# Query transposes by DMA instead of TensorE in a fused pooled-attention and gated-FFN kernel, with a thinner second chunk

## Chip, cores, metric

One core of a Trainium2 chip. The metric is the device time of one execution in microseconds (us), lower is better. Kernels that are compared ran in the same rounds on the same chip. A ratio is the mean time of one kernel's fast runs over the mean of the other's fast runs of the same rounds, so it is not quite the ratio of the medians that are quoted. Spans and times inside a run are from one profiled execution of each kernel.

## The reference, cut to what matters

```python
# q, k, v: [8 batches, 8 heads, 576, 64] float32
k_p = k.reshape(B, H, 72, 8, D).mean(axis=3)      # keys and values pooled by 8
v_p = v.reshape(B, H, 72, 8, D).mean(axis=3)
attn = softmax(q @ k_p.T / sqrt(D))               # 576 x 72 per head
x = (attn @ v_p) as [4608 tokens, 512]
out = (relu(x @ w_gate) * (x @ w_val)) @ w_out    # 512 -> 1536 -> 512
```

## The kernel before

Everything is fp16 in SBUF. The 4608 tokens go through the FFN in 9 chunks of 512. While chunk c runs, the attention of batch c+1 is woven in piece by piece. Scores need the queries with the head dimension on the partitions; they arrive with it along the row, so each batch needs 18 transposes of 128x128, done on TensorE and copied out of PSUM by VectorE.

```python
def load_q(b, ...):                     # cast to fp16 on the way, issued by GpSimd; 2 buffers q16
    nc.gpsimd.dma_start(out=q16_tiles[b][:, cols], in_=flat[:, cols])

def q_transposes(b, n, eng):            # pieces q0, q1 (8 blocks each), q2 (2 blocks)
    if n == 0:
        qT_tiles[b] = qT_pool.tile([P, NI, P], F16, name="qT")          # 2 buffers
    i0, cnt = n * IQ, min(IQ, NI - n * IQ)
    ps = ps_mm.tile([P, IQ, P], F16, name="mm_ps", tag="mm_ps")
    for i in range(cnt):
        c0 = (i0 + i) * P
        nc.tensor.transpose(out=ps[:, i, :], in_=q16_tiles[b][:, c0:c0 + P], identity=ident16)
    ...                                 # copy ps to qT_tiles[b][:, i0:i0 + cnt, :]

def scores(b, h):                       # Sc[h]: 2 matmuls of 288 columns, one Exp on ACT
def values(b, h):                       # V[h]: 2 matmuls of 288 columns, Ln and Exp on ACT,
                                        #       2 multiplies on VectorE into x_T
def attention(b, nxt):
    Sc, V = scores_of(b), values_of(b)
    if nxt is None:
        return [V[0], Sc[2], V[1], ..., Sc[7], V[6], V[7]]               # 14 pieces
    (q0, q1, q2), kt = transposes_of(nxt)
    Sn = scores_of(nxt)
    return [V[0], q0, Sc[2], V[1], Sc[3], V[2], q1, Sc[4], V[3], Sc[5], V[4], kt, Sc[6], V[5],
            Sc[7], V[6], q2, V[7], Sn[0], Sn[1]]

def weave(units, others):               # pieces spread evenly over the units
    n, m = len(others), len(units)
    for i, unit in enumerate(units):
        unit()
        run(others[i * n // m:(i + 1) * n // m])

# chunk 0, tail (loads of the output weights and of batch 2 are issued just ahead of it)
run(z[0:6] + [a[6], q0, a[7], q1, z[6], q2, z[7], kt, a[8], Sc[0], a[9], Sc[1], ...])
...
for c in range(1, n_chunks):
    units = ...                         # 12 gate/value units; from chunk 2 on 8 output units too
    others = []
    if c + 1 < B:
        others = early + attention(c + 1, c + 2 if c + 2 < B else None)   # early: batch 2, chunk 1 only
        early = []
        if c + 2 < B:
            prep(c + 2, c + 3 < B)      # pooling of batch c+2 on GpSimd, loads of batch c+3
        else:
            others += [lambda: None] * 3                                  # fillers
    weave(units, others)
```

The softmax here doesn't subtract the row's maximum and nothing guards it: scores larger than these inputs give would overflow.

Of the kernel before, what the change touches and what calls it, by code (L numbers as in the profile page):

```python
# [10 lines left out]
F16 = mybir.dt.float16  # L11
# [5 lines left out]
def kernel(  # L17
# [10 lines left out]
    nc = tc.nc  # L28

    B, H, S, D = q.shape  # L30
# [5 lines left out]
    P = 128  # L36
# [9 lines left out]
    NI = QT // 2  # L46
# [14 lines left out]
    qT_pool = ctx.enter_context(tc.tile_pool(name="qT", bufs=2))  # L61
# [45 lines left out]
    k_tiles, v_tiles, q16_tiles = {}, {}, {}  # L107
# [56 lines left out]
    def run(pieces):  # L164
        for piece in pieces:
            piece()
# [7 lines left out]
    def k_windows(b, ps, w0, n):  # L174


        for w in range(w0, w0 + n):
            nc.tensor.transpose(
                out=ps[:, w, :],
                in_=kps[b % 2][:KROWS, w:w + 2, :].rearrange("p j d -> p (j d)"),  # L180
                identity=ident16[:KROWS, :KROWS])

    def k_evacuate(b, ps, upper, eng):

        ds, x, w = (slice(D, P), 1, 0) if upper else (slice(0, D), 0, 1)
        dst = kpTs[b % 2].rearrange("d h x (s j) -> d h x s j", j=KJ)[ds, :, x]
        src = ps.rearrange("d w (h s) -> d h s w", h=H)[ds, :, :, w:w + KJ]
        if eng is nc.scalar:
            eng.copy(dst, src)
        else:  # L190
            eng.tensor_copy(out=dst, in_=src)

    def k_transposes(b):
        ps = ps_mm.tile([P, KJ + 1, KROWS], F16, name="mm_ps", tag="mm_ps")
        k_windows(b, ps, 0, KJ + 1)
        for upper in (False, True):
            k_evacuate(b, ps, upper, nc.vector)

    qT_tiles = {}

    def q_transposes(b, n, eng):
        if n == 0:
            qT_tiles[b] = qT_pool.tile([P, NI, P], F16, name="qT")
# [5 lines that stand above are left out]
        dst = qT_tiles[b][:, i0:i0 + cnt, :]  # L209
        if eng is nc.scalar:  # L210
            eng.copy(dst, ps[:, :cnt])
        else:
            eng.tensor_copy(out=dst, in_=ps[:, :cnt])

    def queries(b, h, i0=0, n=NI):
        return qT_tiles[b][:, i0:i0 + n, h * QP:(h + 1) * QP]
# [3 lines left out]
    def scores(b, h):  # L220
        ps = ps_at.tile([P, 2, 512], F32, name="at_ps", tag="at_ps")
        for j in range(2):
            nc.tensor.matmul(  # L223
                out=ps[:SP, j, :HS], lhsT=kpTs[b % 2][:, h, j, :], rhs=queries(b, h),
                start=True, stop=True,
            )
        e = exp_pool.tile([P, 2, HS], F16, name="expT")
        nc.scalar.activation(out=e[:SP], in_=ps[:SP, :, :HS], func=AF.Exp, scale=EXP_SCALE)  # L228
        exp_tiles[b, h] = e
# [226 lines left out]
    def scores_of(b):  # L456
        return [lambda h=h: scores(b, h) for h in range(H)]

    def values_of(b):
        return [lambda h=h: values(b, h) for h in range(H)]  # L460

    def transposes_of(b):
        return [lambda n=n: q_transposes(b, n, nc.vector) for n in range(NQ)], \
            lambda: k_transposes(b)

    def attention(b, nxt):


        Sc, V = scores_of(b), values_of(b)
        if nxt is None:  # L470
            return [V[0], Sc[2], V[1], Sc[3], V[2], Sc[4], V[3], Sc[5], V[4], Sc[6], V[5], Sc[7],
                    V[6], V[7]]
        (q0, q1, q2), kt = transposes_of(nxt)
        Sn = scores_of(nxt)
        return [V[0], q0, Sc[2], V[1], Sc[3], V[2], q1, Sc[4], V[3], Sc[5], V[4], kt, Sc[6], V[5],
                Sc[7], V[6], q2, V[7], Sn[0], Sn[1]]

    def weave(units, others):

# [5 lines left out]
    with tc.manual_schedule():  # L485
        nc.scalar.preload_act_table_set("natural_log_exp_and_others")
        nc.vector.memset(warm_sb, 0.0)
        for kp in kps:
            nc.vector.memset(kp[:, 0, :], 0.0)
            nc.vector.memset(kp[:, KJ + 1, :], 0.0)  # L490
        for kpT in kpTs:
            nc.vector.memset(kpT[:D, :, 1, :], 0.0)
            nc.vector.memset(kpT[D:, :, 0, :], 0.0)
        for st in stats:
            nc.vector.memset(st[:SP, :, D:3 * D], ONE)
        load_k(0, parts=KJ // 2)
        make_identity(nc, ident16)
        load_q(0, 0, IQ)
        load_v(0, (0, D, SP))
        load_gv(0)  # L500
        load_q(0, IQ, NI - IQ)
        for i in range(1, 4):
            load_gv(i)
        load_k(1)
        load_gv(4)
        load_q(1)
        load_gv(5)
        load_v(1)

        for i in range(KJ // 2):  # L510
            run(pool_k(0, i, nc.vector))
        warm(12)
        k_ps = ps_mm.tile([P, KJ + 1, KROWS], F16, name="mm_ps", tag="mm_ps")
        k_windows(0, k_ps, 0, 2)
        warm(3)
        k_windows(0, k_ps, 2, 2)
        warm(2)
        q_transposes(0, 0, nc.scalar)
        k_windows(0, k_ps, 4, KJ - 3)
        k_evacuate(0, k_ps, False, nc.vector)  # L520
        k_evacuate(0, k_ps, True, nc.vector)
        warm(2)
        piece_scores(0)
        warm(2)
        piece_scores(1)
        warm(2)
        pool_v_array(0, 0)
        pool_v_array(0, 1)

        half = TCH // 2  # L530
        a = [lambda fo=fo: gate_val(0, fo, 0, half) for fo in range(n_fo)]
        z = [lambda fo=fo: gate_val(0, fo, half, half) for fo in range(n_fo)]
        piece_values(0)
        piece_values(1)
        warm(1)
        piece_back(0, nc.vector)
        warm(1)
        piece_back(1, nc.scalar)
        a[0]()
        q_transposes(0, 1, nc.scalar)  # L540
        piece_scores(2)
        a[1]()
        q_transposes(0, 2, nc.vector)
        piece_scores(3)
        a[2]()
        piece_values(2)
        piece_scores(4)
        a[3]()
        piece_back(2, nc.vector)
        piece_values(3)  # L550
        a[4]()
        piece_back(3, nc.scalar)
        piece_values(4)
        a[5]()
        piece_back(4, nc.vector)

        for i in range(KJ // 2):
            run(pool_k(1, i, nc.gpsimd))
        for i in range(3):
            load_wo(i, n_fo // 3)  # L560
        load_k(2)
        load_q(2)
        load_v(2)
        (q0, q1, q2), kt = transposes_of(1)
        Sc, V = scores_of(1), values_of(1)
        pv = [lambda half=half: pool_v_array(1, half) for half in range(2)]
        o = [p for ts in range(TCH // P) for p in out_rows(0, ts, nc.vector)]

        run(z[0:6] + [a[6], q0, a[7], q1, z[6], q2, z[7], kt, a[8], Sc[0], a[9], Sc[1], z[8], Sc[2],
                      z[9], Sc[3], a[10], Sc[4], a[11], Sc[5], z[10], Sc[6], z[11], Sc[7]])  # L570
        run(pv + [o[0], V[0], o[1], V[1], o[2], V[2], o[3], V[3], o[4], V[4], o[5], V[5], o[6], V[6],
                  V[7], o[7]])
        prep(2, True)
        (q0, q1, q2), kt = transposes_of(2)
        early = [q0, q1, kt, q2] + scores_of(2)[:2]

        for c in range(1, n_chunks):
            units = []
            for fo in range(n_fo):
                units.append(lambda fo=fo: gate_val(c, fo))  # L580
                if c > 1 and fo % 3:
                    if fo % 3 == 1:
                        parts = out_rows(c - 1, fo // 3)
                    units.append(parts[fo % 3 - 1])
            others = []
            if c + 1 < B:
                others = early + attention(c + 1, c + 2 if c + 2 < B else None)
                early = []
                if c + 2 < B:
                    prep(c + 2, c + 3 < B)  # L590
                else:
                    others += [lambda: None] * 3
            weave(units, others)
        for ts in range(TCH // P - 1):
            run(out_rows(n_chunks - 1, ts))
        last_rows(n_chunks - 1, TCH // P - 1)
# [30 lines left out]
```

## Time and profile before

| | |
|---|---|
| median time (first 3 runs) | 358.71 us (357.07 to 360.11) |
| profiled span, mean granted TensorE clock | 355.9 us, 0.997 |
| TensorE busy | 95% |
| chunks 2 to 5, start to start | 36.34 us each, no hole on TensorE |
| chunk 1, start to start | 33.48 us, of which 5.7 us are holes |

TensorE is the bound. In the trace neighbouring matmuls overlap (at 98.74 us four of 512 columns are shown with 1.03 us, and the next four start 0.86 us later), so what counts is the distance from one start to the next. A "hole" below is the distance between two starts less the issue time of the first. The lines are in the prediction.

### The profile page before, as it was taken

The page shows a single profiled execution, that of the slowest core. Times are in us where ns is not written, and L with a number is a line of the kernel's source. Part 1 is how long each engine was busy: PE and PEld are TensorE (multiplying, and loading weights), DVE is VectorE, ACT ScalarE, POOL GpSimd, SP SyncE. Part 2 cuts the span into 40 slices and gives each one's busy share as a digit, 9 for nine tenths or more (in the row PEclk, how much of TensorE's full clock was granted, in tenths as well). Part 3 has the DMA queues.
Part 4 walks back from the last instruction along what each step waited for, and adds up shares of the span by engine and source line. Part 5 has one row for each costly group of instructions (what it writes and reads, how often), then busy time and mean ns, then how long its engine had stood idle before and what let it go on. Part 6 is the DMA issues. An engine that isn't in the chain of part 4 may idle for free.

```text
span 355.9 us, 5354 instructions
## 1 busy us (share of the span) xinstructions
PE 338.9 (95%) x1993; PEld 181.5 (51%) x1993; DVE 178.1 (50%) x315; ACT 200.4 (56%) x337; POOL 132.5 (37%) x184
## 2 busy tenths in 40 slices
PE   7779999898899999999999999999999999999994
PEld 2567885444445555555555455554554444444443
DVE  6436636655744544454445444453444322289940
ACT  1363468468856676667666666666777333323220
POOL 8448329999999039701996200000000000000000
PEclk9999999999999999999999999999999999999998
DMA  7999996949092427232810111111110111111114
GB/s 111 197 203 197 184 201 102 181 91 182 6 172 59 96 55 139 42 85 39 154 31 19 43 29 31 29 29 31 29 29 18 44 29 31 29 35 45 40 31 117
DMA packets 21594, 28.66 MB, mean 81 GB/s; under 512 B 2432, under 2 KB 14976, under 8 KB 21568
## 3 DMA queue, kind: packets, MB, share of 16 engines
q0 software_dynamic: 16496, 18.88, 32.6%
q1 hardware_dynamic: 4928, 9.31, 10.0%
q8 instruction: 15, 0.25, 0.3%
q10 hardware_dynamic: 144, 0.13, 0.1%
q14 instruction: 11, 0.09, 0.1%
HBM read 37.75 MB, written 9.44 MB: 133 GB/s over the span
## 4 chain that ended last, share of the span: by engine, by line
PE 73%; POOL 13%; DMA 10%; issue 2%; ACT 1%; DVE 0%; POOLq 0%
PE mm_ps L348 42%; PE mm_ps L393 23%; DMA k_in<-in_k_dram 7%; POOL tree_a L139 5%; POOL tree_b L145 3%; PE at_ps L236 3%; PE at_ps L223 3%; DMA v_in<-in_v_dram 2%; PE mm_ps L208 1%; POOL kp L150 1%; POOL stat L150 1%; PE mm_ps L416 1%; POOL k_in L116 1%; POOL wo_sb L440 1%; POOL v_in L123 0%
## 5 line engine op out<-in xcount | busy, mean ns | idle before, releaser
L364 DVE TENSOR_TENSOR h<-mm_ps,relu 128x512 f16<-128x512 f32 (+1 forms) x120 | 96.5, 817 | 102.2 <-PE mm_ps L348 92.3
L348 PE MATMUL mm_ps<-x_T,wg_sb 128*128 128x512 f16 (+1 forms) x480 | 113.2, 358 | 1.3 <-ACT x_T L335 0.7
L348 PE MATMUL mm_ps<-x_T,wv_sb 128*128 128x512 f16 (+1 forms) x480 | 113.0, 358 | 0.0
L393 PE MATMUL mm_ps<-wo_sb,h 128*128 128x512 f16 x420 | 101.1, 379 | 0.0
L354 ACT ACTIVATE relu<-mm_ps 128x512 f16<-128x512 f32 (+1 forms) x120 | 66.4, 553 | 50.8 <-PE mm_ps L348 50.0
L348 PEld LDWEIGHTS <-wv_sb 128*128 128x128 f16 x480 | 46.9, 98 | 47.2 <-issue 0.8
L246 DVE TENSOR_TENSOR x_T<-at_ps,rden 64x512 f16<-64x512 f32 x56 | 38.5, 688 | 52.5 <-ACT rden L244 52.1
L348 PEld LDWEIGHTS <-wg_sb 128*128 128x128 f16 x480 | 46.0, 97 | 33.8 <-issue 1.0
L393 PEld LDWEIGHTS <-h 128*128 128x128 f16 x420 | 40.2, 97 | 40.5
L242 ACT ACTIVATE lg<-at_ps 64x576 f32<-64x576 f32 x56 | 36.1, 645 | 29.0 <-PE at_ps L236 28.7
L228 ACT ACTIVATE expT<-at_ps 72x576 f16<-72x576 f32 x56 | 36.1, 646 | 27.2 <-PE at_ps L223 27.1
L244 ACT ACTIVATE rden<-lg 64x576 f32<-64x576 f32 x56 | 38.1, 681 | 1.8
L145 POOL TENSOR_TENSOR tree_b<-tree_a 72x256 f32<-72x256 f32 (+1 forms) x45 | 32.5, 722 | 3.5
L402 ACT COPY fout<-mm_ps 128x512 f32<-128x512 f32 x31 | 18.2, 586 | 24.9 <-PE mm_ps L393 21.7
L139 POOL TENSOR_TENSOR tree_a<-k_in 96x512 f32<-96x512 f16 x21 | 24.1, 1149 | 15.4 <-DMA k_in<-in_k_dram 15.4
L139 POOL TENSOR_TENSOR tree_a<-v_in 72x512 f32<-72x512 f16 x24 | 27.7, 1153 | 0.1
L223 PE MATMUL at_ps<-qT,kpT 128*72 128x288 f16 x112 | 23.0, 287 | 2.7 <-ACT expT L228 1.2
L236 PE MATMUL at_ps<-expT,stat 72*128 72x288 f16 x112 | 23.0, 286 | 2.5 <-DVE x_T L251 1.6
L223 PEld LDWEIGHTS <-kpT 128*72 128x72 f16 x112 | 12.5, 113 | 13.5 <-issue 2.2
L236 PEld LDWEIGHTS <-stat 72*128 72x128 f16 x112 | 10.6, 98 | 15.9 <-DVE x_T L251 1.4
L131 POOL DMA_DIRECT2D q<-in_q_dram x9 | 5.1, 564 | 32.0 <-PE mm_ps L208 31.4
L150 POOL TENSOR_TENSOR stat<-tree_b 72x128 f16<-72x128 f32 x24 | 10.8, 451 | 10.9 <-PE at_ps L236 9.1
(52 smaller groups left out, 164.2 us busy)
## 6 DMA issues: line engine op xcount, KB each, us to landing
out_dram<-fout SPq DMA_DIRECT2D x31, 256.0 KB
k_in<-in_k_dram POOLq DMA_DIRECT2D x7, 576.0 KB, 6.1
q<-in_q_dram POOLq DMA_DIRECT2D x7, 576.0 KB, 9.3
v_in<-in_v_dram POOLq DMA_DIRECT2D x7, 576.0 KB, 11.9
wg_sb<-in_moe_w_gate_dram POOLq DMA_DIRECT2D x6, 256.0 KB, 10.6
wv_sb<-in_moe_w_val_dram POOLq DMA_DIRECT2D x6, 256.0 KB, 10.7
wo_sb<-in_moe_w_out_dram POOLq DMA_DIRECT2D x3, 512.0 KB, 10.4
out_dram<-fout SPq DMA_DIRECT2D x16, 64.0 KB
```

What stands on the lines that cost most here:

```text
L139: eng.tensor_tensor(out=cell["a"][:n], in0=src[:, :, :4 * D], in1=src[:, :, 4 * D:], op=ALU.add)
L145: eng.tensor_tensor(out=cell["c"][:n], in0=a[:n, :, :2 * D], in1=a[:n, :, 2 * D:], op=ALU.add)
L223: nc.tensor.matmul(out=ps[:SP, j, :HS], lhsT=kpTs[b % 2][:, h, j, :], rhs=queries(b, h), start=True, stop=True,)
L228: nc.scalar.activation(out=e[:SP], in_=ps[:SP, :, :HS], func=AF.Exp, scale=EXP_SCALE)
L236: nc.tensor.matmul(out=ps[:, j, :HS], lhsT=stats[b % 2][:SP, g, hh * P:(hh + 1) * P], rhs=e[:SP, j, :], start=True, stop=True,)
L242: nc.scalar.activation(out=lg[xs], in_=ps[ds, :, :HS], func=AF.Ln)
L244: nc.scalar.activation(out=r[xs], in_=lg[xs], func=AF.Exp, scale=-1.0)
L246: nc.vector.tensor_tensor(out=x_T[xs, g, x0:x0 + FULL].rearrange("p (n j s) -> p j n s", j=2, n=NF), in0=ps[xs, :, :n].rearrange("p j (n s ...
L348: nc.tensor.matmul(out=t[:, :n], lhsT=w[:, ci, fsl], rhs=x_T[:, ci, p0:p0 + n], start=(ci == 0), stop=(ci == n_co - 1),)
L354: nc.scalar.activation(out=relu[:, :n], in_=ps[0][:, :n], func=AF.Relu)
L364: nc.vector.tensor_tensor(out=h, in0=val, in1=relu, op=ALU.mult)
L393: nc.tensor.matmul(out=t, lhsT=h_tiles[c, fo][:, ts * P:(ts + 1) * P], rhs=wo_sb[:, fo, :], start=(fo == 0), stop=(fo == n_fo - 1),)
```

## The change

The intent: transposes of the queries of batches 1 to 7 leave TensorE and VectorE for the DMA engines, which are full for the first 50 us (0.9 or more in the page's slices from 9 to 53 us) and have room later (busy share 0.57 in chunk 1, 0.13 from 246 to 278.6 us, by the prediction's table), and chunk 1, which has no output units between its gate/value units, gets fewer attention pieces.

```diff
+    def q_dma(b):
+        qT_tiles[b] = qT_pool.tile([P, NI, P], F16, name="qT")
+        nc.sync.dma_start_transpose(
+            out=qT_tiles[b], in_=q16_tiles[b].rearrange("p (i d) -> p i d", d=P))
...
+    def firsts_of(b):
+        return [lambda: k_transposes(b)] + scores_of(b)[:2]
+
     def attention(b, nxt):
         Sc, V = scores_of(b), values_of(b)
-        (... the two lists with q0, q1, q2, cut)
+        kt, *Sn = firsts_of(nxt) if nxt else [None]
+        seq = [V[0], Sc[2], V[1], Sc[3], V[2], Sc[4], V[3], Sc[5], V[4], kt, Sc[6], V[5], Sc[7],
+               V[6], V[7]] + Sn
+        return [p for p in seq if p]
...
         load_v(2)
-        (q0, q1, q2), kt = transposes_of(1)
+        q_dma(1)
+        q_dma(2)
...
-        run(z[0:6] + [a[6], q0, a[7], q1, z[6], q2, z[7], kt, a[8], Sc[0], a[9], Sc[1], z[8], Sc[2],
-                      z[9], Sc[3], a[10], Sc[4], a[11], Sc[5], z[10], Sc[6], z[11], Sc[7]])
+        run(z[0:6] + a[6:8] + z[6:7] + [lambda: k_transposes(1), z[7], a[8], Sc[0], a[9], Sc[1],
+                                        z[8], Sc[2], z[9], Sc[3], a[10], Sc[4], a[11], Sc[5],
+                                        z[10], Sc[6], z[11], Sc[7]])
...
-        (q0, q1, q2), kt = transposes_of(2)
-        early = [q0, q1, kt, q2] + scores_of(2)[:2]
...
+            if c + 2 < B:
+                q_dma(c + 2)
             if c + 1 < B:
-                others = early + attention(c + 1, c + 2 if c + 2 < B else None)
-                early = []
+                others = firsts_of(c + 1) if c < 3 else []
+                others += attention(c + 1, c + 2 if 2 <= c < B - 2 else None)
                 if c + 2 < B:
                     prep(c + 2, c + 3 < B)
-                else:
-                    others += [lambda: None] * 3
```

More of the change, by code (lines that the diff above doesn't have):

```diff
@@ L464, in transposes_of @@
             lambda: k_transposes(b)
+    def firsts_of(b):
+        return [lambda: k_transposes(b)] + scores_of(b)[:2]
     def attention(b, nxt):
         Sc, V = scores_of(b), values_of(b)
-        if nxt is None:
-            return [V[0], Sc[2], V[1], Sc[3], V[2], Sc[4], V[3], Sc[5], V[4], Sc[6], V[5], Sc[7],
-                    V[6], V[7]]
-        (q0, q1, q2), kt = transposes_of(nxt)
-        Sn = scores_of(nxt)
-        return [V[0], q0, Sc[2], V[1], Sc[3], V[2], q1, Sc[4], V[3], Sc[5], V[4], kt, Sc[6], V[5],
-                Sc[7], V[6], q2, V[7], Sn[0], Sn[1]]
+        kt, *Sn = firsts_of(nxt) if nxt else [None]
+        seq = [V[0], Sc[2], V[1], Sc[3], V[2], Sc[4], V[3], Sc[5], V[4], kt, Sc[6], V[5], Sc[7],
+               V[6], V[7]] + Sn
+        return [p for p in seq if p]
     def weave(units, others):
```

## The prediction

The +1.0 of (6) is not a worked figure. The 200 GB/s of the loads is the page's own row (184 to 203 in the slices from 9 to 53 us).

> **What bounds the kernel now.** I read the page's busy shares first, then the busy time stretch by stretch, then the TensorE timeline at the ends of the stretches, then the groups and waits of the queries' path, and last the DMA view. The busy shares of the page, with two rows of its slices (DMA and granted clock):
>
> ```profile
> PE 338.9 (95%) x1993; PEld 181.5 (51%) x1993; DVE 178.1 (50%) x315; ACT 200.4 (56%) x337; POOL 132.5 (37%) x184
> ...
> PEclk9999999999999999999999999999999999999998
> DMA  7999996949092427232810111111110111111114
> ```
>
> TensorE is at 95% and everything else near half or below, at full granted clock; the DMA engines are full only in the first 50 us or so. The table of stretches says where the other 5% lies (columns: stretch, its length, then busy us and count for PE, PEld, DVE, ACT and POOL, clock, DMA share, GB/s):
>
> ```profile
> 65.30:98.70 33.40, 28.95 (x183) 15.33 (x182) 21.66 (x41) 23.47 (x38) 31.51 (x43) 1.00 0.57 107
> 98.70:138.00 39.30, 39.30 (x218) 20.18 (x217) 18.07 (x34) 26.51 (x44) 23.73 (x32) 1.00 0.55 105
> 138.00:174.00 36.00, 36.00 (x201) 18.54 (x200) 17.23 (x33) 24.23 (x40) 16.78 (x23) 1.00 0.40 76
> ...
> 246.00:278.60 32.60, 32.60 (x164) 16.09 (x163) 14.61 (x28) 22.27 (x36) 0.00 (x0) 1.00 0.13 32
> ```
>
> From the start of chunk 2 (98.7 us) to the end TensorE has no hole at all: there, time is worth exactly the issue time of its matmuls. Chunk 1 (65.3 to 98.7) has holes: it alone has no output matmuls, only 12 gate/value units of 1.73 us, with 26 attention pieces woven in. Its TensorE timeline (start, duration, group, in brackets the idle time) shows the holes at its end:
>
> ```profile
> 95.97 0.41 PE L236 MATMUL at_ps<-expT,stat 72*128 72x288 f16 x2
> 96.81 0.44 PE L223 MATMUL at_ps<-qT,kpT 128*72 128x288 f16 x2 [0.42 <-DVE qT L213]
> 98.49 0.41 PE L223 MATMUL at_ps<-qT,kpT 128*72 128x288 f16 x2 [1.25 <-ACT expT L228]
> 98.74 1.03 PE L348 MATMUL mm_ps<-x_T,wg_sb 128*128 128x512 f16 x4
> ```
>
> Durations there overlap, so I measure holes from start to start: 512 columns cost 0.216 us, an attention pair 0.245 us. By that, chunk 1 loses 0.72 at its first unit (waiting for the last values of batch 1), 0.64 before the first scores, twice 0.96 and once 0.29 where a values piece waits for the buffer of the one before, and 0.59 + 1.43 in the lines above; with two of 0.05 that is 5.7 us.
>
> The queries' groups, by shape, and two timeline lines:
>
> ```profile
> L208 PE MATMUL mm_ps<-ident,q 128*128 128x128 f16 x144 | 11.8, 219 | 1.0 <-DMA q<-in_q_dram 1.0
> ...
> L213 DVE COPY qT<-mm_ps 128x1024 f16<-128x1024 f16 x14 | 9.4, 676 | 0.0
> ```
>
> ```profile
> 138.78 0.61 PE L208 MATMUL mm_ps<-ident,q 128*128 128x128 f16 x8
> 139.22 1.03 PE L393 MATMUL mm_ps<-wo_sb,h 128*128 128x512 f16 x4
> ```
>
> One transpose lasts 219 ns but eight of them hold the engine from 138.78 to 139.22: 55.6 ns each. The busy column (11.8 us) is not the price; 144 x 55.6 ns = 8.0 us is.
>
> [...]its loads move about 200 GB/s when all DMA engines are busy. [...]loads issued close together land later (6 us alone, 16 in a crowd).
>
> **The change, part by part.**
>
> (1) Removed: 7 x 18 = 126 transposes on TensorE, 126 x 55.6 ns = 7.0 us. All lie where TensorE has no slack: 18 in chunk 0 (36.4 to 39.2 us), 36 in chunk 1, 18 in each of chunks 2 to 5. I count all 7.0. Their 21 VectorE copies go too, some 11 us of an engine at 50%: worth nothing by itself, except at the two places where a qT copy released TensorE (0.64 and 0.59 above), which other waits take over (3).
>
> (2) Chunk 0: the pooled keys' transposes of batch 1 now have two gate units (0.87 us each) before the first scores instead of one. Now TensorE loses 0.9 us there (0.24 + 0.67, first scores at 41.45 and 42.24); with 0.87 more between, some 0.1 remains: -0.8.
>
> (3) Chunk 1 keeps 17 pieces over 12 units. By the weave's indices: keys after unit 0, first scores after unit 1, values 0 to 7 after units 2, 4, 5, 7, 8, 9, 11, 11. Holes that I expect: 0.72 at the start, unchanged; 0.4 before the first scores (the two key copies end 2.4 us after the key transposes start, 2.0 us of work lies between); values pieces one unit apart (4 to 5, 7 to 8, 8 to 9) have 2.2 us between starts, and one needs about 2.75 (0.45 to ACT, 0.65 + 0.68 there, 0.69 + 0.21 on DVE): 3 x 0.55 = 1.65. And at the end both last values pieces come after the last unit, with nothing behind them but chunk 2's first unit, which reads their result: 0.41 latency, 4 ACT passes of 0.66, then 0.7 on DVE = 3.8 us, against 1.15 us of work: 2.7. Sum 5.5 against 5.7 before: -0.2. So thinning out this chunk buys nearly nothing, because the last two pieces lose their cover.
>
> (4) Moved to chunk 2: keys and first two scores of batch 3 (0.79 us of TensorE, same work, no gain), with a new wait of 0.4 between them as in (3): +0.4. Values lie two units apart there (3.5 us): no hole, as now.
>
> (5) Chunk 6: the three empty fillers at its end go, so 14 pieces spread over all 20 units, and the last values piece falls after the last unit instead of three units earlier. Chunk 7's first unit needs it (64 tokens of batch 7). From that piece's start: 0.85 us until the output copy frees ACT, 1.33 of Ln and Exp, 0.9 on DVE = 3.1 us; work to cover it: 0.25 + three matmuls of 0.216 = 0.9. New hole: +2.2.
>
> (6) The transposing DMA of batch 1. Its load lands late, as the DMA view of the window 19.0 to 20.2 us shows (last column: us from issue, at 19.65, to landing):
>
> ```profile
> q<-in_q_dram POOLq DMA_DIRECT2D x1, 576.0 KB, 13.2
> ```
>
> So it can start at 32.85. The first scores of batch 1 will be due at about 41.45 - 1.0 (transposes gone) - 0.25 = 40.2. It has 7.3 us. [...] I put in +1 for the chance of a miss. For batches 2 to 7 there is a chunk (over 30 us) of lead.
>
> (7) The SP queue issues the output stores too, in order. Batch 2's queries land at 37.6 + 16.4 = 54.0, so chunk 0's stores, now first issued at 56.5, go behind that transpose; with three output buffers a store may be some 5 us late without harm. +0.1.
>
> (8) GpSimd's wait for a query buffer (from the table of waits) goes away:
>
> ```profile
> POOL q L131 <- PE mm_ps L208: 31.4, 2, 17.3
> ```
>
> It cost TensorE nothing after 98.7, so nothing is gained.
>
> Sum: -7.0 - 0.8 - 0.2 + 0.4 + 2.2 + 1.0 + 0.1 = -4.3 us. From 358.7: **354.4 us**, 1.2% faster.
>
> **The rivals.**
> A. The full removal arrives: (1) and (2) and none of the new holes, 358.7 - 7.8 = 350.9, just past 2%. For it: ACT and DVE have slack on average. Against: (3) and (5) are chains with nothing between, and the start of chunk 1 shows such a one already (0.72, with an output block behind the last values piece).
> B. The DMA transpose is slow. [...] At 12 us for one transpose the wait is 4.6 and the buffers cost about 2: about 360. Nothing in the profile of before speaks for or against[...].
> C. The transposes crowd the loads. 576 KB more in a stage at 200 GB/s delays what follows by 3 us: the output weights (last part lands at 48.5, needed at 53.5) and keys of batch 2 (landing 51.3, pooled by 58.7, needed at 65.8) have 5 us and more: 354 still; if it takes thrice that, 357.
>
> **Range and chances.** The core is 351 to 357, set by holes (3), (5) and the miss of (6); the tail to the right is B, which I give one chance in five, most of it past +2%; the left is A with chunk 1 going better than my chain says. Range 349.5 to 364. Faster by over 2% needs 351.5 or less: 0.21. Within 2%: 0.65. Slower: 0.14.
>
> **What would show it.** Right: no query transposes on TensorE but batch 0's 18; from chunk 2 on the chunks shorter by 1.0 us each in chunks 2 to 5; first scores of batch 1 near 40 us with at most a small hole ahead; a hole of 2 to 3 us at the start of chunk 2's and of chunk 7's first unit, released by DVE's x_T; chunk 1 about 3.0 us shorter, 2.8 of it through work removed (2.0) and moved (0.8), not through holes. Wrong: batch 1's first scores waiting for the DMA (a transpose longer than 7 us, landing after 40); output copies waiting for stores near 65 us; holes in chunk 1 under 3 us (then A); holes at other chunk ends that I don't foresee.

## The result, and the profile after

The changed kernel takes 375.07 us in the median of 4 runs (373.47 to 376.51), the kernel before 358.11 beside it. The ratio is 1.0465, 95% interval 1.0398 to 1.0532: 4.7% slower. The profiled span is 372.7 us.

The page of the changed kernel, busy shares and two rows of its 40 slices:

```profile
PE 339.5 (91%) x1867; PEld 178.7 (48%) x1867; DVE 169.2 (45%) x294; ACT 201.3 (54%) x337; POOL 132.5 (36%) x184
...
PEclk9969956999998999999999999999999899999999
DMA  7999998799959385575141014111110101111104
```

TensorE has 126 instructions fewer, as it should, but is busy for a smaller share. The sixth and seventh slices of the clock (about 47 to 65 us) show it reduced while TensorE idled and just after. The TensorE timeline there (start, duration, group, idle time before it and what ended it):

```profile
41.73 0.60 PE L354 MATMUL mm_ps<-x_T,wv_sb 128*128 128x256 f16 x4
58.45 0.64 PE L229 MATMUL at_ps<-qT,kpT 128*72 128x288 f16 x2 [16.12 <-DMA qT<-q]
58.88 1.06 PE L354 MATMUL mm_ps<-x_T,wg_sb 128*128 128x256 f16 x4
59.73 1.06 PE L354 MATMUL mm_ps<-x_T,wv_sb 128*128 128x256 f16 x4
```

In the kernel before, the same place looked like this:

```profile
42.24 0.31 PE L223 MATMUL at_ps<-qT,kpT 128*72 128x288 f16 x1 [0.48 <-DVE kpT L191]
...
43.51 0.60 PE L348 MATMUL mm_ps<-x_T,wg_sb 128*128 128x256 f16 x4
43.94 0.60 PE L348 MATMUL mm_ps<-x_T,wv_sb 128*128 128x256 f16 x4
```

Batch 1's first scores waited 16.1 us for its DMA transpose. For 4.9 us after it the matmuls ran at half speed: groups of four of 256 columns start 0.85 us apart in place of 0.43. From these first scores to the fourth took 5.71 us against 3 x 1.12 = 3.36 in the kernel before: 2.35 us more. The transpose had been issued when I said it could be, on the SP queue:

```profile
32.85 6.36 SPq L218 DMA_TRANSPOSE qT<-q  x1
```

What the DMA queues did from 33 to 58.5 us in the changed kernel (queue, packets, MB, share of 16 engines; q0 carries the loads, q1 the SP queue; the shares add up to more than 100%, so packets of the two overlap in time):

```profile
q0 software_dynamic: 2933, 2.74, 87.4%
q1 hardware_dynamic: 2336, 0.59, 48.6%
```

and from 188 to 196 us, around a later transpose with no load beside it, but with an output store of the same queue, which ends 1.2 us after the transpose's first packet:

```profile
q1 hardware_dynamic: 2472, 0.85, 54.6%
...
out_dram<-fout SPq DMA_DIRECT2D x1, 256.0 KB
qT<-q SPq DMA_TRANSPOSE x1
```

A transpose is 2304 packets of 256 bytes (and 32 of 4 bytes); spread evenly that is 144 for each of the 16 engines, though the records do not name the engine. By the trace's packet records, this one took 5.5 us from issue to the last packet: 2.0 until the first, 3.5 for the packets. Batch 1's took 24.2 us, first to last 22.5; the other five took 4.9 to 7.4 us, those of chunk 1 with some loads beside them. Beside it the loads fared badly too: the output weights' landing went from 10.4 us (the page of before) to

```profile
wo_sb<-in_moe_w_out_dram POOLq DMA_DIRECT2D x3, 512.0 KB, 25.6
```

Two more places, at the first unit of chunk 2 and of chunk 7:

```profile
111.06 0.81 PE L354 MATMUL mm_ps<-x_T,wg_sb 128*128 128x512 f16 x3
114.53 0.59 PE L354 MATMUL mm_ps<-x_T,wg_sb 128*128 128x512 f16 x1 [2.66 <-DVE x_T L252]
114.91 1.92 PE L354 MATMUL mm_ps<-x_T,wv_sb 128*128 128x512 f16 x4
...
292.18 0.81 PE L354 MATMUL mm_ps<-x_T,wg_sb 128*128 128x512 f16 x3
295.10 0.38 PE L354 MATMUL mm_ps<-x_T,wg_sb 128*128 128x512 f16 x1 [2.11 <-DVE x_T L257]
295.32 1.80 PE L354 MATMUL mm_ps<-x_T,wv_sb 128*128 128x512 f16 x4
```

These are the holes that the prediction gave to the last values pieces, with something added: after each of them four matmuls of 512 columns take 1.6 to 1.7 us in place of 0.86, again a reduced clock (0.50 for 3.41 us in the trace's clock records).

Where the time came from, by starts on TensorE (lengths in us; holes and reduced clock from start to start):

| stretch | before | after | what makes the difference |
|---|---|---|---|
| to the start of chunk 1 | 65.26 | 83.92 | hole 16.1, reduced clock after it 2.35; reduced clock near 20 us 2.0 (see below); -1.8 of transposes and a wait gone |
| chunk 1 | 33.48 | 27.14 | 2.0 of transposes, 0.8 moved on; holes 5.7 to 2.2 |
| chunk 2 | 36.34 | 40.59 | hole 2.82, reduced clock 1.65; 0.8 moved in, 1.0 removed |
| chunks 3, 4, 5 | 36.34 each | 35.33 each | 1.0 of transposes each |
| chunk 6 | 34.54 | 34.54 | |
| chunk 7 | 31.08 | 35.04 | hole 2.27, reduced clock 1.69 |
| chunk 8, output units | 41.36 | 41.36 | |
| the rest, to the end of the span | 4.8 | 4.1 | not followed |

The reduced clock near 20 us lies ahead of every changed instruction. It is in the profiles of seven of the twelve kernels here (the third slice of the clock row), with and without transposing DMA, and other runs of the kernel before have mean clocks from 0.981 to 1.000. It differs from run to run, lasted 6.8 us in the changed kernel (0.50 from 18.9 to 25.8 us) and cost it 2.0, and is not an effect of the change.

### The profile page after: what moved, and what is told of

Its sections match the earlier page's. It is cut to its first block, busy times and chain, and to the rows that moved or that the text cites. A ratio compares the mean times of both kernels' runs of the same rounds, so it can differ in the third digit from the quotient of the medians.

```text
span 372.7 us, 5113 instructions
## 1 busy us (share of the span) xinstructions
PE 339.5 (91%) x1867; PEld 178.7 (48%) x1867; DVE 169.2 (45%) x294; ACT 201.3 (54%) x337; POOL 132.5 (36%) x184
## 5 line engine op out<-in xcount | busy, mean ns | idle before, releaser
L354 PE MATMUL mm_ps<-x_T,wg_sb 128*128 128x512 f16 (+1 forms) x480 | 116.6, 365 | 6.0 <-DVE x_T L257 2.7
L354 PE MATMUL mm_ps<-x_T,wv_sb 128*128 128x512 f16 (+1 forms) x480 | 116.6, 367 | 0.0
L354 PEld LDWEIGHTS <-wv_sb 128*128 128x128 f16 x480 | 48.1, 100 | 54.2 <-issue 8.2
L354 PEld LDWEIGHTS <-wg_sb 128*128 128x128 f16 x480 | 47.2, 100 | 35.8 <-issue 2.4
L229 PE MATMUL at_ps<-qT,kpT 128*72 128x288 f16 x112 | 23.8, 294 | 16.3 <-DMA qT<-q 16.1
L408 ACT COPY fout<-mm_ps 128x512 f32<-128x512 f32 x31 | 18.1, 585 | 31.4 <-PE mm_ps L399 28.4
L191 DVE COPY kpT<-mm_ps 64x576 f16<-64x576 f16 x16 | 12.0, 750 | 0.9 <-PE mm_ps L178 0.7
## 6 DMA issues: line engine op xcount, KB each, us to landing
v_in<-in_v_dram POOLq DMA_DIRECT2D x7, 576.0 KB, 12.8
wo_sb<-in_moe_w_out_dram POOLq DMA_DIRECT2D x3, 512.0 KB, 25.6
```

The costliest lines, as they stand in the source:

```text
L229: nc.tensor.matmul(out=ps[:SP, j, :HS], lhsT=kpTs[b % 2][:, h, j, :], rhs=queries(b, h), start=True, stop=True,)
L354: nc.tensor.matmul(out=t[:, :n], lhsT=w[:, ci, fsl], rhs=x_T[:, ci, p0:p0 + n], start=(ci == 0), stop=(ci == n_co - 1),)
```

## The experiments

The disputed question was why batch 1's transpose took three to five times as long as the later ones. My theory: crowding, that is, the loads beside it stretch the time of each of its many small packets. The rivals: a one-time cost of the first transposing DMA, sharing by bytes, a cost that any load brings whatever its amount. A second question was what the new order of pieces costs by itself.

### 1. Batch 1 back on TensorE

```diff
-        q_dma(1)
+        (q0, q1, q2), _ = transposes_of(1)
         q_dma(2)
-        run(z[0:6] + a[6:8] + z[6:7] + [lambda: k_transposes(1), ...
+        run(z[0:6] + [a[6], q0, a[7], q1, z[6], q2] + [lambda: k_transposes(1), ...
```

> The changed kernel with batch 1's queries transposed on TensorE again (18 transposes and 3 copies in chunk 0), batches 2 to 7 by DMA. Theory (batch 1's DMA transpose takes 25 us[...]): the 16.1 us hole before batch 1's first scores goes, and with it some 2.3 us of reduced clock after it; 1.0 us of transposes comes back: 372.7 - 17.4 = about 355 us span, level with before or up to 1% faster. The transpose of batch 2, now the first to be issued, lands within 10 us of its load. Rival (the first DMA transpose of a program pays a one-time cost of some 20 us, whatever else runs): the transpose of batch 2 then takes 25 us from 54, and batch 2's first scores, due near 68, wait until 79: a hole of 11 us, 366 us.

Measured: 356.44 us, ratio to before 0.995 (0.9884 to 1.0016), span 354.8. The hole is gone. Batch 2's transpose, now the first of the program, was issued at 53.52 on the SP queue

```profile
53.52 3.89 SPq L218 DMA_TRANSPOSE qT<-q  x1
```

and its last packet ended at 59.05: 5.5 us, like the later ones. So there is no one-time cost here, and the 18.6 us between the medians (of different rounds, in which the kernel before took 358.1 and 358.9) hang on this one transpose. The holes of 2.82 and 2.27 us at chunks 2 and 7 are here as well, reduced clock included, and eat much of what the transposes gain. The program's third transpose, from 91 us, ran with no other packet beside it (SP queue's timeline, and the DMA queues from 91 to 95.5 us):

```profile
91.03 2.69 SPq L218 DMA_TRANSPOSE qT<-q  x1
...
q1 hardware_dynamic: 2336, 0.59, 69.6%
```

It took 4.1 us from issue, 2.9 of them from the first packet to the last: this, not 5.5, is the time of a transpose quite alone here (0.59 MB in 2.9 us, 203 GB/s).

### 2. Batch 1 by DMA, the competing loads held until it has landed

```diff
+        q_dma(1)
+        hold = const_pool.tile([P, 2], F16, name="hold")
+        nc.gpsimd.tensor_copy(out=hold, in_=qT_tiles[1][:, NI - 1, :2])
         for i in range(3):
             load_wo(i, n_fo // 3)
         load_k(2)
...
-        q_dma(1)
         q_dma(2)
```

> The changed kernel with the loads of the output weights and of batch 2 held back until batch 1's transpose has landed (a GpSimd copy of two columns of its result stands before them). Theory (crowding): only the load of batch 1's values is left beside the transpose, so it lands within 10 us of 32.85, by 43, and the hole before batch 1's first scores is under 2 us; the output weights land near 52 and may cost 1 to 3 us there; span 355 to 359. Rival (one-time or per-block cost of the transpose itself): it takes 25 us as before, the hole stays near 16 us and the held loads add more: over 375.

Measured: 356.98 us, ratio 0.9958 (0.9879 to 1.0036, 2 runs), span 354.7. The wait of the held loads, from the table of waits, and the holes on TensorE:

```profile
POOL hold L567 <- DMA qT<-q: 7.3, 1, 7.3
```

```profile
42.09 0.40 PE L229 MATMUL at_ps<-qT,kpT 128*72 128x288 f16 x2 [0.84 <-DMA qT<-q]
54.76 1.02 PE L399 MATMUL mm_ps<-wo_sb,h 128*128 128x512 f16 x4 [0.71 <-DMA wo_sb<-in_moe_w_out_dram]
...
70.01 1.02 PE L354 MATMUL mm_ps<-x_T,wg_sb 128*128 128x512 f16 x4 [1.02 <-DVE fout L406]
```

With the rest of one load (batch 1's values) beside it, the same transpose takes 8.8 us instead of 24.2. It is the loads. The third line is the output-buffer wait of the prediction's step (7): chunk 0's stores stood in the SP queue behind batch 2's transpose, issued at 60.36 (the first store is issued at 64.27), and it cost 1.0, not 0.1.

### 3. The fillers of chunk 6 put back

```diff
                     prep(c + 2, c + 3 < B)
+                else:
+                    others += [lambda: None] * 3
```

> The changed kernel with the three empty fillers of chunk 6 put back, nothing else. Theory: the last values piece gets three units of cover again, the 2.1 us hole at chunk 7's first unit goes, and the reduced clock in the 4 us after it too (1.7 us): 3.8 us less than the changed kernel, about 369 us span, ratio to before 1.036. Rival (the slow matmuls after that hole come from something else, such as a clock that drops at about that time anyway): only 2.1 us less, with slow matmuls still near 295 us.

Measured: 370.21 us, ratio to before 1.0313 (1.0246 to 1.0379), span 368.9, three fast runs and a slow one, which is not counted. Chunk 7 is back at 31.08 us: hole and reduced clock both went, 3.96 us. In this pair of profiles the reduced clock went with the hole (that it does not always follow one, see the sixth experiment). The first scores of batch 1 in this run:

```profile
58.97 0.64 PE L229 MATMUL at_ps<-qT,kpT 128*72 128x288 f16 x2 [19.11 <-DMA qT<-q]
```

TensorE reached them 2.5 us earlier than in the changed kernel's profile (no reduced clock near 20 us), and the data came at about the same time (58.97 and 58.45): there the DMA sets the pace, and what TensorE saves ahead of it is lost in the hole.

### 4. Half of batch 1's blocks by DMA

```diff
-        q_dma(1)
+        qT_tiles[1] = qT_pool.tile([P, NI, P], F16, name="qT")
+        nc.sync.dma_start_transpose(          # blocks 0 to 8; blocks 9 to 17 on TensorE
+            out=qT_tiles[1][:, :9, :], in_=q16_tiles[1][:, :9 * P].rearrange("p (i d) -> p i d", d=P))
         q_dma(2)
```

> The changed kernel with 9 of batch 1's 18 blocks by DMA, 9 on TensorE. Theory ([...]its time goes with its packets): half of 25.5 us, 12.8 us from 32.85, landing near 45.6; batch 1's first scores are due near 42.0, so the hole is 3 to 5 us; span near 360. Rival (a fixed cost of the first transpose): still 20 us and more, hole 12 to 16 us, span near 371.

Measured: 359.22 us, ratio 1.002 (0.9935 to 1.0105, 2 runs), span 356.4.

```profile
42.92 0.41 PE L229 MATMUL at_ps<-qT,kpT 128*72 128x288 f16 x2 [2.25 <-DMA qT<-q]
```

Half the packets took 9.2 us from issue, less than half of 24.2; I had said 12.8. So not a fixed cost, but not proportional either: the second half of the whole transpose is the slower one. It falls in the time in which batch 2's loads follow (where in it, see the fifth experiment).

### 5. Only batch 2's loads held, the output weights' beside the transpose

```diff
             load_wo(i, n_fo // 3)
+        q_dma(1)
+        hold = ...                            # as in the second experiment
         load_k(2)
```

> The changed kernel with only batch 2's loads held behind batch 1's transpose; the three output-weight loads (1536 packets of 1 KB) stay beside it. Theory ([...]the half transpose, 73 packets an engine, took 9.6 us beside the weights' loads, so 131 ns a packet): the whole one takes 146 x 131 = 19 us while loads last, landing at 46 to 53, hole of 5 to 11 us, span 360 to 366. Rival 1 (the queues share by bytes, about 200 GB/s in all): 0.59 MB of transpose beside as many bytes of load, 6 to 8 us, landing by 42, no hole over 2 us. Rival 2 (the slowness comes with any load at all, whatever its amount): landing near 58 as in the changed kernel.

Measured: 367.99 us, ratio 1.0244 (1.0181 to 1.0306, 2 runs), span 367.3.

```profile
52.52 0.64 PE L229 MATMUL at_ps<-qT,kpT 128*72 128x288 f16 x2 [12.10 <-DMA qT<-q]
```

The last packet came 18.4 us after the issue, the landing at 52.5, in the window I gave; the hole was 1 us and the span 1.3 us over mine. Sharing by bytes (by 42) and a cost whatever the amount (58) are both out. The doses, with the time from the first packet to the last divided by 144 packets an engine:

| beside batch 1's transpose | issue to last packet | per packet |
|---|---|---|
| nothing (batch 4, first experiment) | 4.1 us | 20 ns |
| the end of an output store (a later batch, changed kernel) | 5.5 us | 24 ns |
| rest of one load | 8.8 us | 51 ns |
| that and the output weights, 9 blocks only | 9.2 us | 108 ns (72 packets) |
| that and the output weights, all 18 blocks | 18.4 us | 118 ns |
| that and batch 2's loads (the changed kernel) | 24.2 us | 156 ns |

In the packet records of these stretches a 256-byte packet of the transpose mostly takes 18 or 31 ns, a 1 KB packet of the loads 96 to 98, one of 4.6 KB 360, one of 6 KB 473. An estimate of mine from these records: one packet of the transpose and one of 1 KB together take 114 to 129 ns, near the 108 and 118 ns seen beside the output weights. The counts fit it roughly: in the changed kernel, from the transpose's first packet to its last, its 2304 packets ran beside 2108 of the loads, 271 of which are 4-byte ones, so about 0.8 load packets with data for each. In what order the packets of the two queues ran was not shown, since the records do not name the engine of a packet. Nor did any run change the size of the loads' packets at the same bytes.

The estimate covers most of the 24.2 us, not all. In the changed kernel 982 transpose packets start between 42 and 49 us, one per 114 ns and engine, and by 50.0, 17 us after the issue, 91% have started; the fifth experiment had 94% by then. What batch 2's loads add is the end: the last 209 packets take 7 us more. In these 7 us 65 packets of 4.6 and 6 KB started beside them. And of the 16 landings of each output-weight load in the changed kernel, the last four come 4.0 to 9.4 us after the twelfth (0.3 to 1.7 in the kernel before). Whether either holds the last packets back was not shown.

### 6. The order of pieces alone, no transposing DMA

The kernel before with the changed order: query pieces put back at their old places beside the new lists, batch 3's first pieces at the start of chunk 2, no fillers.

```diff
-        q_dma(1)
-        q_dma(2)
+        (q0, q1, q2), _ = transposes_of(1)    # and q pieces in attention() and firsts_of(), no q_dma
```

> No transposing DMA at all: the kernel before with the changed kernel's order of pieces only (17 pieces plus batch 2's four query pieces in chunk 1, batch 3's first pieces at the start of chunk 2, no fillers in chunk 6). Theory: it loses. Chunk 0 gains 0.8; chunk 1's holes are about equal, but the 2.7 us hole at chunk 2's first unit brings 1.6 us of reduced clock after it; chunk 6 brings a hole of 2.1 and 1.7 of reduced clock: about 4 us slower than before, ratio 1.008 to 1.015. Rival: the thinner chunk 1 is a gain by itself, ratio under 1.000.

Measured: 363.16 us, ratio 1.0125 (1.0083 to 1.0168), span 360.4. The number is as expected, the working only partly. The holes on TensorE in the profiled run, the fastest of the six:

```profile
72.49 0.40 PE L229 MATMUL at_ps<-qT,kpT 128*72 128x288 f16 x2 [1.24 <-DVE qT L213]
...
97.48 0.38 PE L354 MATMUL mm_ps<-x_T,wg_sb 128*128 128x512 f16 x1 [2.68 <-DVE x_T L252]
105.71 0.41 PE L229 MATMUL at_ps<-qT,kpT 128*72 128x288 f16 x2 [0.94 <-DVE qT L213]
...
284.01 0.38 PE L354 MATMUL mm_ps<-x_T,wg_sb 128*128 128x512 f16 x1 [2.11 <-DVE x_T L257]
```

The two holes behind the last values pieces are there, but this profiled run shows no reduced clock after them: chunk 7 is 2.28 us longer than before, not 3.96. In its place come waits for the query copies that VectorE makes at the start of chunks 1 and 2. So holes of 2.3 to 2.8 us came with a reduced clock after them in one profile and without in another.

The clock records show this much of when it did. In the changed kernel all of them but the last are 3.41 us long or a whole multiple of it (half clock for 6.83, 17.07, 3.41 and 3.41 us, from 18.94, 46.24, 114.51 and 295.42 us). Two stretches of the changed kernel around chunk 2's hole, then two of this kernel (length, TensorE busy; third from the end is the granted clock):

```profile
111.10:114.50 3.40, 0.77 (x4) 0.25 (x3) 1.96 (x5) 2.56 (x4) 3.31 (x6) 1.00 1.27 155
114.50:117.90 3.40, 3.37 (x14) 1.57 (x14) 1.09 (x3) 0.60 (x1) 3.17 (x5) 0.50 1.00 202
...
92.40:95.80 3.40, 2.26 (x12) 1.01 (x11) 1.98 (x4) 3.30 (x6) 3.17 (x5) 1.00 0.00 0
95.80:99.20 3.40, 1.72 (x14) 1.03 (x14) 1.58 (x5) 1.46 (x3) 0.60 (x2) 1.00 0.63 94
```

In the changed kernel one stretch holds the whole hole, 83% of its length, and the next runs at 0.50; at chunk 7 the hole of 2.27 us lies in one stretch too (292.0 to 295.4 us, 67% of it), and the next has 0.50. In the sixth experiment a cut at 95.8 splits the hole in two, holes fill 43% and 49% of the two stretches, and the clock stays at 1.00. In the second experiment's profile the matmuls after chunk 2's hole keep their full pace (two of 512 columns in 0.43 us from 99.70 us), those after chunk 7's do not (four in 1.59 us from 277.38). What share of a stretch is needed was not shown, and holes alone do not decide it: before 18.9 us the changed kernel has holes of 0.39, 0.30 and 0.67 us and then half clock, the kernel before has the same three and keeps 1.00. I take the 1.6 to 1.7 us to be a matter of luck from run to run; other runs of the sixth kernel have mean clocks down to 0.987 and may have paid them, but no profile of them shows it.

### 7. Batch 1 on TensorE, and cover for the last values pieces

```diff
                     prep(c + 2, c + 3 < B)
+                if c == 1 or c + 2 >= B:
+                    others += [lambda: None] * 3
```

on top of the first experiment.

> Batch 1 on TensorE, batches 2 to 7 by DMA (as in the first experiment), and three empty fillers at the end of chunk 1 and of chunk 6, so that the last values pieces have units behind them. Theory: the 2.7 and 2.1 us holes and the reduced clock after them (1.6, 1.7) go, at the price of about 1 to 2 us of small holes in the denser chunk 1: 354.8 - 6 = about 349 us span, ratio to before 0.970 to 0.980. Rival: chunk 1 gives all of it back through waits on ACT, ratio 0.985 or more.

Measured: 349.55 us (348.14 to 350.93), ratio 0.972 (0.9683 to 0.9757), span 349.1. Chunk 1 takes 28.06 us with 3.1 us of small holes (2.2 without fillers), chunk 2 36.46 (40.6 without), chunk 7 31.08. Ratio and span are as I expected. This is the best of all the kernels by the median, 2.8% faster than before.

### 8. The same cover, batch 1 by DMA with the loads held

> The same fillers, with all seven batches by DMA and the loads held behind batch 1's transpose. Theory: 1.0 us of transposes less than the kernel with batch 1 on TensorE, but about 2.5 us of small waits (transpose, output weights, output buffers): 0 to 2 us slower than that one, ratio to before 0.973 to 0.985. Rival: the waits hide elsewhere and it is the fastest of all, by 1 us.

Measured: 350.06 us, ratio 0.9745 (0.9711 to 0.9778), span 348.6. The waits found in the second experiment (0.87, 0.49 and 1.12 us here) stand against the 1.0 us of transposes saved; the intervals of this kernel and the last overlap, so the two cannot be told apart.

### 9 and 10. The two parts of the gain, separated

The ninth kernel is the sixth with the fillers of the seventh: all transposes on TensorE. The tenth is the first with the order of before: `firsts_of` in chunk 1 only, batch 3's first pieces at the end of chunk 1, fillers in chunk 6.

> All transposes on TensorE, the changed order of pieces, and the fillers at the ends of chunks 1 and 6. Theory: the two holes of 2.7 and 2.1 us that the order alone had (1.2% slower than before) are covered, 4 to 5 us: level with before, ratio 0.994 to 1.004. The difference to the kernel with the same order and batches 2 to 7 by DMA (0.972) is then what these transposes are worth: 108 x 55.6 ns = 6.0 us by issue time alone (1.7%), more if the query copies also held TensorE up. Rival: the order with fillers is itself most of the gain, ratio under 0.985.

> Batch 1 on TensorE, batches 2 to 7 by DMA, all pieces in the order of before (batch 3's first pieces at the end of chunk 1, fillers in chunk 6). Theory: 6.0 us of transposes and 0.8 in chunk 0 go; chunk 1 keeps a hole of 1 to 2 us at its end, where the fillers had none: ratio 0.974 to 0.984. Rival: without the query pieces the old order is as good as the covered one, 0.972 or less; then thinning chunk 1 was for nothing.

Measured: the ninth 359.71 us, ratio 1.0015 (0.997 to 1.0061); the tenth 350.0 us, ratio 0.9749 (0.9706 to 0.9793). The end of chunk 1 in the tenth:

```profile
95.35 0.44 PE L229 MATMUL at_ps<-qT,kpT 128*72 128x288 f16 x2 [0.33 <-DVE x_T L257]
96.75 0.44 PE L229 MATMUL at_ps<-qT,kpT 128*72 128x288 f16 x2 [0.96 <-DVE x_T L257]
```

| ratio to before | order of before | order of the change | that with fillers |
|---|---|---|---|
| batches 2 to 7 on TensorE | 1 | 1.0125 | 1.0015 |
| batches 2 to 7 by DMA, batch 1 on TensorE | 0.9749 | 0.995 | 0.972 |
| all seven by DMA (the change) | not run | 1.0465 | not run |

The gain comes from the DMA of batches 2 to 7 (2.5 and 3.0%, but only 1.7% in the order of the change, where its profile has the reduced clock twice and that of the kernel without DMA has not), the loss from batch 1's and from the new order without fillers (1.3 to 2.0%). With fillers the new order is no better than the old one beyond the intervals. By starts on TensorE, chunks 1 and 2 together have 5.7 us of holes before and 4.4 in the tenth, 8.4 in the ninth and 3.4 in the seventh: the transposes' removal is worth its issue time (6.0 us) plus 1.3 us of holes in the old order and 5.0 in the new one.

## Why the prediction was wrong, point by point

- **(6) The transposing DMA of batch 1 is the step that failed.** It stood in the sum as +1.0, an allowance for a miss of the 7.3 us that it had; the estimate of its length behind that rested on a bandwidth that no trace here shows, and took the sharing with the loads to be by bytes. With no load beside it, a transpose does take 4.1 to 5.5. But in 256-byte packets beside packets of 1 KB and more it took 24.2 us, some 17 of them covered by the estimate of the fifth experiment, and the term measured 16.1 of hole and 2.35 of reduced clock: 18.5. One fact was at hand: the DMA row was full until about 50 us (and not only then, as the prediction reads it: the same row has slices of 0.9 near 67, 85 and 102 us, and the later transposes had a whole chunk to hide behind). What I lacked was the size of a transpose's packets and what they cost beside others. In the packet counts of before nothing shows it.
- **Rival B, a slow DMA transpose, is what came:** 24.2 us, and 16.1 of wait. Its main case rested on a time for a block that no trace here shows. Quite alone, a block took 2.9 us / 18 = 0.16. It also expected loss through output buffers (about 2 us), and of that the changed kernel shows none, since TensorE itself was late.
- **Rival C** asked what the transpose does to the loads, and they did land later (weights 25.6 in place of 10.4 us), without any effect in the changed kernel, again since TensorE stood still.
- **(1) 7.0 us of transposes: right.** Chunks 3 to 5 are shorter by 1.01 us each. That their VectorE copies are worth nothing except at the two places named was right within 1.3 us for the old order; the sixth and ninth kernels show waits for them of 0.9 to 1.2 us.
- **(2) The wait for the keys in chunk 0:** no such hole is left in the changed kernel. Its 0.8 us could not be seen as time, since the DMA hole follows.
- **(3) Chunk 1: right in sum and in its main line.** Expected 5.5 us of holes with 2.7 at the end, measured 2.2 + 2.8 = 5.0.
- **(4) +0.4 was not found** in the changed kernel; 0.3 in the seventh.
- **(5) Hole at chunk 7: 2.2 expected, 2.27 measured.** Missing in (3) and (5) was the reduced clock after the holes, 1.65 and 1.69 us in the changed kernel.
- **(7)** was hidden in the changed kernel, and mis-sized where it shows (1.0 for 0.1, second experiment).
- **(8)** was right: the wait for a query buffer fell from 31.4 to 5.0 us and nothing came of it.

The first experiment's kernel has all the other steps. By the prediction's terms it takes 1.0 less (no chance of a miss) and 1.0 more (batch 1's transposes), a gain of 4.3 us again; in its rounds it gained 1.8 (0.5%; by the interval from 4.2 gained to 0.6 lost), with 3.3 us of reduced clock after the two holes in its profile. So the rest of the working held but for this clock, as far as the noise lets one tell.

## What to carry to other kernels

Here a DMA of 2304 packets of 256 bytes took 4.1 us alone (first experiment) and 24.2 beside bulk loads, and TensorE waited 16.1 us for it. Before putting such a DMA beside loads when something waits for it, count its packets per engine and multiply by what one packet of it and one of the neighbour take together in the trace, instead of dividing its bytes by a bandwidth (an estimate: 144 x some 120 ns = 17 us, a lower bound here, where 24 came). A transpose also held the queue that issues it for 2.6 to 6.4 us in the changed kernel (4.45 in the median), and an output store behind one cost TensorE 1.0 us in the second experiment. Moving work off the bounding engine paid its issue time where a lead of a whole stage hid the replacement (batches 2 to 7, 2.5 and 3.0%); the first use, with no lead, was better left where it was, or the loads beside it held back, which came out level (seventh and eighth experiments). When pieces are thinned out or fillers dropped, look at what then stands last before the stage that reads it: here 2 to 3 us of bare latency at each such end outweighed the tidier middle.
